# K K^T of chunks 6 to 11 in four-bank visits, the solve over two chunks, and U over four corners

## The chip, the core and the metric

The kernel runs on one core of a Trainium2 chip. The core has a matrix engine (TensorE, PE in the profile, with PEld for its weight loads), a vector engine (DVE), a scalar engine (ACT), GpSimd (POOL) and SyncE (SP), which here only issues DMAs; POOL issues DMAs too. Matmuls write to PSUM, which is handed out in banks of 128 x 512 fp32. The metric is the device time of one execution in microseconds, as the median of three runs.

## The reference

Four batches, eight heads, 768 tokens, heads of 48: a delta rule over the tokens, whose output, rearranged to 3072 x 384, goes through two MLPs.

```python
k_n = k / (norm(k) + 1e-06)
for t in range(S):
    y[:, :, t] = einsum('bhd,bhde->bhe', q[:, :, t], state)
    v_old = einsum('bhde,bhd->bhe', state, kt)
    state = state + bt * einsum('bhd,bhe->bhde', kt, vt - v_old)
x = y.transpose(0, 2, 1, 3).reshape(B * S, H * D)
h = np.maximum(x @ w_in, 0.0)                    # d_ff 2048
x = h * h @ w_out
h = np.maximum(np.maximum(x @ w1, x @ w2), x @ w3)   # d_ff 768
return h @ w_out2
```

## The kernel before

The tokens are cut into 12 chunks of 64 (`NC`). Within a chunk the delta rule is solved at once: K K^T of the chunk's keys, with beta, gives a triangular system of 64 x 64 per head, and its inverse is built from 32 x 32 blocks (the **solve**). All 32 heads are worked on together, in two halves p = 0 and 1 of eight pairs of heads (`U2` is 8; the two heads of a pair lie at partitions 0 to 63 and 64 to 127, t = 0 and 1). Chunks go in pairs: `HALVED[g]` is chunks 2g and 2g + 1, and the solve of a pair is done in one go, since 128 partitions hold both.

The MoE of a chunk, `moe_a(c)`, is the main stream of TensorE. For each of eight pairs of ff-tiles, `s1` does 18 matmuls 128 x 256 (L599), ACT and DVE square the result and split it into gh and gl (L605 to L608), and `s2` does 12 matmuls 128 x 384 (L619), two pairs later. `moe_a` yields after each s1 and each s2, and `steps` (L655 on) calls other generators at these yields by lists of numbers, the **slots**: 1 is behind s1(0), 2 behind s1(1), 3 behind s1(2), 4 behind s2(0), 5 behind s1(3), 6 behind s2(1), and so on by turns, to 12 behind s2(4), 13 behind s1(7), 14 behind s2(5), 15 behind s2(6), 16 behind s2(7) and the two DVE transposes of its sums (L639), which SP stores in the next chunk (`store_sums`, L652, the x stores). In the program's order these are the only places at which small work enters the stream. The orders of TensorE and DVE are pinned to the program's (`pin`); the queues of SP, ACT and POOL are laid out by the framework.

What is put into the slots of chunk c:

- `attention(c + 1)`, seven steps: load; A and Y from the state (`st0`, L467, 64 matmuls to each of two p, pA from pool `ps_at`, pY from `ps_y`); `zz` (L426); `ww` (L436); `mm_u`, the product U (L491, L494), whose result is copied to SBUF by ACT for p = 0 (L503) and by DVE for p = 1 (L501); `st2`, which adds P U to pY and gets the state's growth pD (L543, L521, L528, copies L553); and `st3`, transposes of the output (L561) that ACT and DVE split into xh and xl (L564, L565) for the next chunk's s1.
- `kkps`, K K^T of a pair of chunks, half by half: load of the keys (L169, 448 KB, two buffers in `buf` and `big`), `kk_matmul` (L172 to L182) into two banks pk and pq, copy by ACT (L198) and multiply by the mask on DVE (L199), stores kk (L186) and p (L206) to DRAM.
- `solve32` of the pair: loads of M from kk_d (L312), `prep` on DVE (L247 to L255, with a root on ACT, L218, and a select on POOL, L236), the transposed norms pt on TensorE (L279), 30 steps of two DVE instructions (L292, L293), the last multiply L296, and the stores of xt (L329), from which POOL loads xb and x for the attention.

K K^T of pair g stands in chunk 3, 5 and 7 for the pairs 3, 4 and 5 (`KK`), in four visits of two banks at slots 4, 6, 8 and 9. The solve's loads stand at slot 11, its prep at slot 15, and its steps in slots 1 to 14 of the next, even chunk. `ps_at` and `ps_y` have two banks each, px (two banks, sums of s2) and the two double banks of s1 take the others; U finds spare columns ("corners") of px and pY behind the 384 in use: four of eight heads of p = 0 lie in px, two of p = 1 in pY of p = 1.

Of the kernel before, what the change touches and what calls it, by code (L numbers as in the profile page):

```python
# [17 lines left out]
B, H, S, D = 4, 8, 768, 48  # L18
C = 64
# [4 lines left out]
DM = H * D  # L24
# [11 lines left out]
HALVED = [(c, c + 1) for c in range(0, NC, 2)]  # L36
U2 = 2 * Q


def delta_moe(ctx, tc, kc, ab, kt, vt, beta, beta32, beta16, kq, w_in, w_out, w1, w2, w3, w_out2, out):  # L40
    nc = tc.nc
    vec, act, pool = nc.vector, nc.scalar, nc.gpsimd
# [14 lines left out]
    ps_at = pp.enter_context(tc.tile_pool(name="ps_at", bufs=2, space=PSUM))  # L57
    ps_y = pp.enter_context(tc.tile_pool(name="ps_y", bufs=2, space=PSUM))
# [5 lines left out]
    mask = const.tile([128, C], F32, name="mask", tag="mask")  # L64
# [3 lines left out]
    p_d = [dram.tile([128, B * Q, C], F32, name=f"p{c}", tag=f"p{c}") for c in range(NC)]  # L68
# [82 lines left out]
    kcts, kss = [], []  # L151
# [7 lines left out]
    kcs, nk, kk_ends, mul_after, kc_after = {}, [0, 0], [None, None], [], []  # L159

    def two(d, c, p):

        return d[:, c, 2 * p:2 * p + 2]

    def kkp_load(c, p, dma=nc.sync):
        k = kcts[nk[0] % len(kcts)]
        nk[0] += 1
        kcs[c, p] = k
        i = dma.dma_start(k, two(kc, c, p).rearrange("p b q t s -> p (b q) t s"))  # L169
        for j in kc_after:  # L170
            behind(i.ins, j)

    def kk_matmul(c, p, ps_, swap=1):

        k = kcs.pop((c, p))
        pk, pq = (ps_[0].tile([128, U2, C], F32, name=n, tag=ps_[1]) for n in ("pk", "pq"))
        for u in range(U2):
            for i, ps in enumerate((pk, pq)):
                for t in range(2):
                    r = slice(64 * t, 64 * t + D)  # L180
                    o = 64 * (t ^ i * swap)
                    pe.matmul(ps[o:o + 64, u], k[r, u, 0], k[r, u, i], start=True, stop=True)  # L182
        return pk, pq

    def kk_store(c, p, kk, dma=nc.sync):
        dma.dma_start(kk_d[c // 2].rearrange("t j c u i -> (t j) c u i")[:, c % 2, U2 * p:U2 * p + U2], kk)  # L186

    def kkps(cs, ps_, dma=nc.sync):

        todo = [(c, p) for c in cs for p in range(2)]  # L190
        ahead = len(kcts) - (len(kcts) < 4)
        for n in range(min(ahead, len(todo))):
            kkp_load(*todo[n], dma)
        for n, (c, p) in enumerate(todo):
            ks = kss[nk[1] % len(kss)]
            nk[1] += 1
            pk, pq = kk_matmul(c, p, ps_[n % len(ps_)])
            kk_ends[0] = act.copy(ks[:, 0], pk).ins  # L198
            kk_ends[1] = vec.tensor_mul(out=ks[:, 1], in0=pq, in1=mask.unsqueeze(1).broadcast_to([128, U2, C])).ins  # L199
            for i in mul_after:  # L200
                behind(kk_ends[1], i)
            yield
            kk_store(c, p, ks[:, 0], dma)

            for t in range(2):
                dma.dma_start(p_d[c][64 * t:64 * t + 64, U2 * p:U2 * p + U2], ks[64 - 64 * t:128 - 64 * t, 1])  # L206
            if n + ahead < len(todo):
                kkp_load(*todo[n + ahead], dma)
            yield


    def norms(ss, n, u, pool_):

# [59 lines left out]
    def behind(ins, before):  # L273

        tc.add_manual_dep(ins, before.name, mybir.DependencyInfo(mybir.DependencyClass.NoSync, mybir.DependencyReason.DATA), reason="order")
# [115 lines left out]
    pxs = []  # L391
    ops, normed, norms_at, solved, solve_after = [], [], [], [], []

    def attention(c):
        xh[c] = wa.tile([128, KD, TB], F32R, name="xh", tag="xh", bufs=2)
        xl[c] = wa.tile([128, KD, TB], F32R, name="xl", tag="xl", bufs=2)
        half = lambda t: slice(64 * t, 64 * t + 64)
# [4 lines left out]
        def fresh(name, p, i, shape):  # L402
            t = att.tile(shape, F32, name=name, tag=name)
            tiles[c, p][i] = t
            return t


        merge, pYs = [], {}
# [69 lines left out]
        def mm_u(p):  # L478
            x, r = tiles[c, p][2], tiles[c, p][6]
            pU = ps_at.tile([128, U2, D], F32, name="pU", tag="at")  # L480
            own = p or c <= 2
            n = U2 - (0 if not c else 2 if own else 4)
            if c:
                free = pYs[p] if own else pxs
                over = free[0].rearrange("p (b n) -> p b n", b=1) if own else free[0]
                over = over[:, :, DM:DM + 2 * D].rearrange("p b (u d) -> p b u d", d=D)
            order = [u for i in range(U2) for u in (i, n + i) if (i < n if u == i else u < U2)]
            for u in order:
                for t in range(2):
                    if u < n:  # L490
                        pe.matmul(pU[half(t), u], x[half(t), u], r[half(t), u], start=True, stop=True)  # L491
                    else:
                        o = over[half(1 - t), (u - n) // 2, (u - n) % 2]
                        i = pe.matmul(o, x[half(t), u], r[half(t), u], start=False, stop=True, skip_group_check=True)  # L494
                        for j in free[1:]:
                            behind(i.ins, j)
            u_ = fresh("u", p, 7, [128, U2, D])
            on_vec = p and c != 1
            def put(to, po):
                if on_vec:  # L500
                    last_vec[0] = vec.tensor_copy(to, po).ins  # L501
                else:
                    last_act[0] = act.copy(to, po).ins  # L503
            put(u_[:, 0:n], pU[:, 0:n])
            if held and c < 2:
                masked(p)
            if c:
                for m in range(n, U2, 2):
                    for t in range(2):
                        put(u_[half(t), m:m + 2], over[half(1 - t), (m - n) // 2])  # L510

        yy, pDs = {}, {}

# [218 lines left out]
    if True:  # L732
# [14 lines left out]
        for t in range(2):  # L747
            m = mask[64 * t:64 * t + 64]
# [44 lines left out]
        at, p1 = (ps_at, "at"), (ps_s1, "p1")  # L793
# [11 lines left out]
        for c in range(2):  # L805
            for x in range(4):
                j = (pool if c else nc.sync).dma_start(halves[0][32 * x + 16 * c:32 * x + 16 * c + 16], beta32[c, 16 * x:16 * x + 16]).ins
# [63 lines left out]
        for n, (c, p) in enumerate(todo):  # L871
            pg = pw[:, 1].rearrange("p (u s) -> p u s", s=C) if n == 1 else bank((sy, None, p1, at)[n])
            grams(n, 1, [pg] * 2)
            ks = kss[n][:, 1] if c else tiles[c, p][3]
# [87 lines left out]
        KK = {1: 2, 3: 3, 5: 4, 7: 5}  # L962
        ahead_ = {}
        for c in range(NC):
            extra = []
            if c == 0:
                solve_next = solve32(1, (pool, pool))
                extra += [(11 / 15.0, later(3, attention(1))), (list(range(17)), weights(2, 2)), (4.0, later(20, part(solve_next, 10)))]
            elif c == 1:
                pinned.update({first_matmul.ins.engine: None, last_gl[0].engine: None})  # L970
                first_solve = [0] * 3 + [1 + n * 18 // 20 for n in range(20)]
                extra += [(first_solve, solve_next), ([13, 19, 22, 25, 27, 28, 30], attention(2))]
                ahead_[2] = solve32(2, landing=1)
                extra += [([9, 10, 16, 17, 20, 21, 24, 25], kkps(HALVED[2], (at,))), ([28], ahead_[2], True)]
                solve_after[:] = last_vec
                kc_after[:] = raws[-1:]
                prep_after.clear()
            elif c + 1 < NC:
                extra.append(([1, 2, 5 + c // 9, 7 + c // 9, 10, 12, 14] if c % 2 else [1, 2, 4, 6, 8, 11, 13], attention(c + 1)))
            if c == 2:  # L980
                kc_after.clear()
                solve_after.clear()
            if c in ahead_:
                extra.append(([2] + [3 + n * 12 // 32 for n in range(32)] if c == 2 else [1 + n * 14 // 32 for n in range(32)], ahead_[c]))
            if c > 1 and c in KK:
                extra.append(([4, 5, 6, 7, 8, 9, 9, 10], kkps(HALVED[KK[c]], (at,))))
                ahead_[c + 1] = solve32(KK[c], landing=1)
                extra.append(([11, 15], ahead_[c + 1], True))
            if c == 9:
                after[:] = last_gl  # L990
                load_w3s = w3load((0, 1))
            if 9 <= c < NC - 1:
                extra.append((0.4, part(load_w3s, 6)) if c > 9 else (0.8, later(6, part(load_w3s, 6))))
            if c == NC - 1:
                pr.close()
                wb = ctx.enter_context(tc.tile_pool(name="wb", bufs=1, side="right", reuse_waits="tile"))
                first = []
                extra.append((0.6, chain(load_w3s, w3load((2,)))))
                extra.append((0.5, later(2, x2_steps(0, wb, first))))
            steps(moe_a(c, gp, c == 1), *extra)  # L1000
# [114 lines left out]
```

## Time and profile before

| | |
|---|---|
| median of three runs | 906.56 us (905.05 to 907.78) |
| profiled execution | 903.85 us, span 902.1 us, mean granted clock 0.977 |
| PE busy | 868.1 us (96%) |
| DVE busy | 479.4 us (53%) |
| ACT busy | 387.7 us (43%) |
| POOL busy | 135.8 us (15%) |
| chunk 7 of the MoE (with K K^T) | 47.41 us |
| chunk 9 (without) | 42.21 us |

The attention with chunk 0 and the load of the weights take the first 120 us or so, the chunks of the MoE run to 597 us, and the second MLP follows. The shares are means over these stages; what a microsecond is worth in one is read from that stage's own waits.

### The profile page before, as it was taken

Reading aid. Unit: us, or ns where it says so; the run is one execution under the profiler, and the core shown is the slowest. Engines: PE = TensorE matmul, PEld = TensorE weight load, DVE = VectorE, ACT = ScalarE, POOL = GpSimd, SP = SyncE. Lnnn points to the kernel's source line nnn. Section 1 sums busy time; section 2 is a strip of 40 time slices with the busy share of each in tenths; the row PEclk is TensorE's granted clock in tenths of the full one; section 3 lists DMA queues with packets and bytes.
Section 4 is the critical chain, followed back from the end, with each engine's and each line's share of the span. In section 5 each row is a group of like instructions: output and inputs, shape, how many; then the busy total and the mean of one; then the engine's idle time right before and its main releaser. Section 6 shows DMA issues by size and latency. Waiting matters only on the chain.

```text
span 902.1 us, 26366 instructions
## 1 busy us (share of the span) xinstructions
PE 868.1 (96%) x11414; PEld 843.6 (94%) x11414; DVE 479.4 (53%) x1069; ACT 387.7 (43%) x825; POOL 135.8 (15%) x226
## 2 busy tenths in 40 slices
PE   5589999999999999999999999999999999999998
PEld 5478989999999999999999999999999999999997
DVE  5988885695378437843784545556232332323221
ACT  5558745354445444534453755644121221212111
POOL 4140200322312241224123300011000000000000
PEclk8659999999999999999999999999999999999999
DMA  9977436725742585257427431444010110000000
GB/s 258 361 184 225 132 89 176 153 65 140 194 112 66 144 191 110 66 145 159 100 66 171 118 92 38 127 111 136 20 36 27 36 37 25 10 27 9 18 18 35
DMA packets 114035, 95.36 MB, mean 106 GB/s; under 512 B 69880, under 2 KB 95240, under 8 KB 113920
## 3 DMA queue, kind: packets, MB, share of 16 engines
q1 hardware_dynamic: 95232, 55.41, 23.8%
q0 software_dynamic: 11584, 32.64, 13.7%
q10 hardware_dynamic: 7104, 5.64, 2.1%
q8 instruction: 89, 1.46, 0.7%
q14 instruction: 26, 0.21, 0.1%
HBM read 70.45 MB, written 22.77 MB: 103 GB/s over the span
## 4 chain that ended last, share of the span: by engine, by line
PE 86%; DVE 6%; ACT 3%; DMA 3%; issue 2%; POOL 0%; DVEq 0%; ACTq 0%; POOLq 0%
PE p L1023 25%; PE p L599 21%; PE px L619 20%; PE po L1040 8%; PE pY L543 2%; PE pU L491 2%; PE pk L182 1%; PE pA L467 1%; DMA p<-ksr 1%; PE pW L436 1%; PE pZ L426 1%; DVE gl L608 1%; PE pT L561 1%; DMA ktp<-in_kt_dram 1%; PE pq L182 1%
## 5 line engine op out<-in xcount | busy, mean ns | idle before, releaser
L1023 PE MATMUL p<-x_h,w 128*128 128x384 f32 x864 | 220.1, 336 | 0.0
L619 PE MATMUL px<-wout,gh 128*128 128x384 f32 x768 | 198.6, 339 | 1.4 <-ACT gh L607 1.4
L599 PE MATMUL p<-xh,win_h 128*128 128x256 f32 x576 | 169.6, 294 | 1.9 <-DVE gl L608 1.4
L599 PE MATMUL p<-xl,win_h 128*128 128x256 f32 x576 | 163.8, 284 | 0.2 <-DVE xl L565 0.2
L599 PE MATMUL p<-xh,win_l 128*128 128x256 f32 x576 | 163.7, 284 | 0.0
L1023 PEld LDWEIGHTS p<-x_h,w 128*128 128x128 f32 x864 | 156.3, 188 | 0.0
L1023 PE MATMUL p<-x_l,w 128*128 128x384 f32 x432 | 145.3, 336 | 0.0
L608 DVE TENSOR_TENSOR gl<-p,gh 128x512 fp32r<-128x512 f32 x96 | 66.3, 690 | 142.3 <-ACT gh L607 141.9
L619 PEld LDWEIGHTS px<-wout,gh 128*128 128x128 f32 x768 | 134.5, 189 | 2.6 <-ACT gh L607 1.5
L619 PE MATMUL px<-wout,gl 128*128 128x384 f32 x384 | 128.8, 335 | 0.0
L605 ACT ACTIVATE p<-p 128x512 f32<-128x512 f32 x96 | 55.9, 583 | 165.1 <-PE p L599 162.6
L599 PEld LDWEIGHTS p<-xh,win_h 128*128 128x128 f32 x576 | 110.6, 192 | 5.8 <-DVE gl L608 2.3
L599 PEld LDWEIGHTS p<-xl,win_h 128*128 128x128 f32 x576 | 110.8, 192 | 0.5 <-DVE xl L565 0.4
L599 PEld LDWEIGHTS p<-xh,win_l 128*128 128x128 f32 x576 | 110.9, 192 | 0.0
L1029 DVE TENSOR_TENSOR mx<-p,mx 128x384 f32<-128x384 f32 x48 | 26.7, 557 | 126.2 <-PE p L1023 126.1
L1023 PEld LDWEIGHTS p<-x_l,w 128*128 128x128 f32 x432 | 81.3, 188 | 0.0
L1031 ACT CAST hh<-mx 128x384 fp32r<-128x384 f32 x48 | 24.6, 514 | 125.4 <-DVE mx L1030 125.2
L619 PEld LDWEIGHTS px<-wout,gl 128*128 128x128 f32 x384 | 72.1, 188 | 0.0
L293 DVE TENSOR_TENSOR buf<-buf 128x30 f32<-128x30 f32 (+9 forms) x180 | 59.7, 332 | 6.1
L292 DVE TENSOR_TENSOR buf<-buf 128x30 f32<-128x30 f32 (+9 forms) x180 | 59.3, 330 | 4.8
L607 ACT CAST gh<-p 128x512 fp32r<-128x512 f32 x96 | 56.3, 587 | 2.5
L606 ACT ACTIVATE p<-p 128x512 f32<-128x512 f32 x96 | 56.0, 583 | 2.6
(169 smaller groups left out, 1309.2 us busy)
## 6 DMA issues: line engine op xcount, KB each, us to landing
kq<-in_kc_dram POOLq DMA_DIRECT2D x20, 448.0 KB, 5.4
raw<-in_moe_w_dram SPq DMA_DIRECT2D x18, 384.0 KB, 3.8
raw<-in_moe_w_out_dram SPq DMA_DIRECT2D x16, 384.0 KB, 3.8
p<-p POOLq DMA_DIRECT2D x22, 256.0 KB, 4.0
rawp<-in_moe_w_in_dram SPq DMA_DIRECT2D x12, 384.0 KB, 6.5
v<-in_vt_dram POOLq DMA_DIRECT2D x24, 192.0 KB, 3.9
ktp<-in_kt_dram POOLq DMA_DIRECT2D x24, 192.0 KB, 4.1
x<-xs SPq DMA_DIRECT2D x48, 96.0 KB, 3.2
```

What stands on the lines that cost most here:

```text
L292: eng.tensor_tensor(out=tv, in0=col.unsqueeze(2).broadcast_to([u, k, l]), in1=row.unsqueeze(1).broadcast_to([u, k, l]), op=ALU.mult)
L293: i = eng.tensor_tensor(out=of_, in0=of_, in1=tv, op=ALU.add)
L599: pe.matmul(p1[:, j], w[:, k, f], x[c][:, k], start=n == 0 and j == 0, stop=n == 8, skip_group_check=True)
L605: act.activation(out=p1, in_=p1, func=AF.Relu)
L606: act.activation(out=p1, in_=p1, func=AF.Square)
L607: last_gh[0] = act.copy(gh, p1).ins
L608: last_gl[0] = vec.tensor_sub(out=gl, in0=p1, in1=gh.bitcast(F32)).ins
L619: g = pe.matmul(px[:, h, 0:DM], x[:, j, hs], w, start=f == 0 and i == 0, stop=f == NF - 1 and i == 2, skip_group_check=True)
L1023: pe.matmul(p, w[i][:, k, fs], x[:, k], start=n == 0, stop=n == 8)
L1029: vec.tensor_max(out=t, in0=ps[1], in1=t)
L1031: act.copy(hh[:, f], t2)
L1040: pe.matmul(po[:, 0:DM], x[:, f, js], w[:, f], start=i == 0, stop=i == 17)
```

## The change

A new generator, `kk_twos`, does K K^T of one chunk in one visit: both halves' keys are loaded, both `kk_matmul` follow one another, p = 0 into the two banks of `ps_at` and p = 1 into those of `ps_y`, then come the copies and multiplies, and at the next call the stores and the loads for the pair's second chunk. The first chunk of a pair is done at slot 15 of the even chunk ahead (its keys are loaded at slot 8), the second at slot 2 of the odd chunk, ahead of A, which moves from slot 2 to 4 there. The solve's loads move from slot 11 to 6 and prep from 15 to 9; seven steps of the solve follow in slots 10 to 16, the others in slots 1 to 12 of the even chunk. pt, which was called at slot 4 with zz, is now called at slot 1. In `mm_u` of p = 1, from chunk 3 on, four of the eight heads go to corners: two in pY of p = 0 and two in pY of p = 1.

```diff
+    def kk_twos(cs):
+        for c in cs:
+            for p in range(2):
+                kkp_load(c, p)
+            yield
+            staged = []
+            for p, ps_ in enumerate(((ps_at, "at"), (ps_y, "y"))):
+                staged.append((kss[nk[1] % len(kss)], *kk_matmul(c, p, ps_)))
+                nk[1] += 1
+            for ks, pk, pq in staged:
+                act.copy(ks[:, 0], pk)
+                vec.tensor_mul(out=ks[:, 1], in0=pq, in1=mask.unsqueeze(1).broadcast_to([128, U2, C]))
+            yield
+            for p, (ks, _, _) in enumerate(staged):
+                kk_store(c, p, ks[:, 0])
+                for t in range(2):
+                    nc.sync.dma_start(p_d[c][64 * t:64 * t + 64, U2 * p:U2 * p + U2], ks[64 - 64 * t:128 - 64 * t, 1])
+        yield
...
-            own = p or c <= 2
-            n = U2 - (0 if not c else 2 if own else 4)
-            if c:
-                free = pYs[p] if own else pxs
+            free = [] if not c else [pYs[p]] if c <= 2 else [pYs[0], pYs[1]] if p else [pxs]
...
+            n = U2 - 2 * len(overs)
...
-                extra.append(([1, 2, 5 + c // 9, 7 + c // 9, 10, 12, 14] if c % 2 else [1, 2, 4, 6, 8, 11, 13], attention(c + 1)))
+                extra.append(([1, 2, 6, 8, 10, 12, 14] if c > 8 and c % 2 else [1, 4, 6, 8, 10, 12, 14] if c % 2 else [1, 2, 4, 6, 8, 11, 13], attention(c + 1)))
...
-                extra.append(([2] + [3 + n * 12 // 32 for n in range(32)] if c == 2 else [1 + n * 14 // 32 for n in range(32)], ahead_[c]))
+                extra.append(([2] + [3 + n * 12 // 32 for n in range(32)] if c == 2 else [1 + n * 12 // 25 for n in range(25)], ahead_[c]))
+            if c > 1 and c + 1 in KK:
+                two_by_two = kk_twos(HALVED[KK[c + 1]])
+                extra.append(([8, 15, 16], two_by_two, True))
             if c > 1 and c in KK:
-                extra.append(([4, 5, 6, 7, 8, 9, 9, 10], kkps(HALVED[KK[c]], (at,))))
+                extra.append(([2, 3], two_by_two))
                 ahead_[c + 1] = solve32(KK[c], landing=1)
-                extra.append(([11, 15], ahead_[c + 1], True))
+                extra.append(([6, 9, *[10 + n for n in range(7)]], ahead_[c + 1], True))
```

The new lines push the others down: L295 on stand 20 lines lower in the new file, `mm_u` and what follows 21.

SP's queue at the end of chunk 2 and the start of chunk 3, before; the first row is the last of four stores of xt (the solved pair 2), x are the sums of chunk 2, kk and p the products of chunk 6. A number in square brackets is the semaphore of a queue or an engine that is waited for.

```order
L329 DMA xt_113<-buf 32x1024 [waits DMAHW1_49]
L652 DMA x_120<-xs 768x1x32 [waits DMAHW2_49,DVE_49]
L652 DMA x_120<-xs 768x1x32 [waits DMAHW3_49]
L652 DMA x_120<-xs 768x1x32 [waits DMAHW4_49]
L652 DMA x_120<-xs 768x1x32 [waits DMAHW5_49]
L169 DMA buf<-in_kc_dram 112x1024 [waits DMAHW6_49,PE_49]
L186 DMA kk_96<-buf 128x512 [waits DMAHW7_49,Activation_49]
L206 DMA p_105<-buf 64x512 [waits DMAHW0_49,DVE_49]
L206 DMA p_105<-buf 64x512 [waits DMAHW1_49]
```

The same place after:

```order
L349 DMA xt_113<-buf 32x1024 [waits DMAHW1_49]
L186 DMA kk_96<-buf 128x512 [waits DMAHW2_49,Activation_49]
L229 DMA p_105<-buf 64x512 [waits DMAHW3_49,DVE_49]
L229 DMA p_105<-buf 64x512 [waits DMAHW4_49]
L186 DMA kk_96<-big 128x512 [waits DMAHW5_49,Activation_49]
L229 DMA p_105<-big 64x512 [waits DMAHW6_49,DVE_49]
L229 DMA p_105<-big 64x512 [waits DMAHW7_49]
L169 DMA buf<-in_kc_dram 112x1024 [waits DMAHW0_49,PE_49]
L169 DMA big<-in_kc_dram 112x1024 [waits DMAHW1_49,PE_49]
L673 DMA x_120<-xs 768x1x32 [waits DMAHW2_49,DVE_49]
```

The stores of both halves of chunk 6 now follow the stores of xt, behind them stand the two loads of chunk 7, and the stores of x come later.

DVE in chunk 3, from the copies of U (L501) to the first row of prep (L247), before; ss, s, r and a are prep's small tiles:

```order
L501 COPY u<-pU 128x288 [waits PE_49]
L501 COPY u<-pY 64x96 x2
L608 TENSOR_TENSOR gl<-p_3778,gh 128x512 [waits PE_49,Activation_49]
L528 TENSOR_TENSOR Sb<-pD,Sb 128x384 [waits PE_49] x2
L553 COPY yy<-pY 64x4x48 x4
L608 TENSOR_TENSOR gl<-p_3914,gh 128x512 [waits DVE_49,PE_49,Activation_49]
L565 TENSOR_TENSOR xl<-pT,xh 128x3x128 [waits Activation_49] x2
L247 COPY ss<-buf 128x32 [waits DMAHW6_49,DMAHW7_49,DMAHW1_49,DMAHW0_49]
```

After, from the end of prep (its multiply by r, L257, and L275) on:

```order
L257 TENSOR_TENSOR buf<-buf,r 128x1024 [waits DVE_49,Pool_49]
L275 TENSOR_SCALAR a_3625<-r 128x32
L522 COPY u<-pU 128x192 [waits PE_49]
L522 COPY u<-pY 64x96 x2
L522 COPY u<-pY 64x96 [waits PE_49]
L522 COPY u<-pY 64x96
L312 TENSOR_TENSOR buf<-buf 128x30 [waits DVE_49]
L313 TENSOR_TENSOR buf<-buf 128x30 [waits DVE_49]
L629 TENSOR_TENSOR gl<-p_3807,gh 128x512 [waits PE_49,Activation_49]
```

Prep stood behind xl; now it stands ahead of the copies of U, which are five in place of three, and of gl.

TensorE at the start of `st2` of p = 0, in chunk 3, before (u are the copied U, p the masked products):

```order
L543 MATMUL pY<-u,p 64x48 [waits DMASW1_49]
L543 MATMUL pY<-u,p 64x48
L521 MATMUL pD<-u,ktp_136 64x48 [waits DMASW2_49,PE_49]
L521 MATMUL pD<-u,ktp_136 64x48
L543 MATMUL pY<-u,p 64x48 x2
```

After:

```order
L564 MATMUL pY<-u,p 64x48 [waits DMASW1_49,DVE_49]
L564 MATMUL pY<-u,p 64x48
L542 MATMUL pD<-u,ktp_136 64x48 [waits DMASW2_49,PE_49]
L542 MATMUL pD<-u,ktp_136 64x48
L564 MATMUL pY<-u,p 64x48 x2
```

The first matmul into pY, which waited for one load alone, waits for DVE too.

## Rows read from the trace of the kernel before

**Rows 1.** The page, busy time (us, share, instructions) of each engine.

```profile
PE 868.1 (96%) x11414; PEld 843.6 (94%) x11414; DVE 479.4 (53%) x1069; ACT 387.7 (43%) x825; POOL 135.8 (15%) x226
```

**Rows 2.** By stretch, chunks 7 and 9: length; PE, PEld, DVE, ACT, POOL; clock, DMA.

```profile
388.54:435.95 47.41, 47.41 (x952) 45.09 (x952) 18.62 (x37) 21.40 (x45) 16.87 (x27) 1.00 0.72 163
...
478.23:520.44 42.21, 42.21 (x697) 40.80 (x696) 19.06 (x40) 24.05 (x50) 15.55 (x26) 1.00 0.62 155
```

**Rows 3.** PE's timeline (start, length) around A, K K^T and U.

```profile
392.56 0.28 PE L599 MATMUL p<-xl,win_h 128*128 128x256 f32 x1
...
395.01 0.28 PE L599 MATMUL p<-xh,win_l 128*128 128x256 f32 x1
...
398.96 0.34 PE L619 MATMUL px<-wout,gl 128*128 128x384 f32 x1
...
400.54 0.28 PE L599 MATMUL p<-xh,win_l 128*128 128x256 f32 x1
...
456.61 0.34 PE L619 MATMUL px<-wout,gl 128*128 128x384 f32 x1
...
458.40 0.28 PE L599 MATMUL p<-xh,win_l 128*128 128x256 f32 x1
```

**Rows 4.** PE's timeline: the last s2 of chunk 2, A in chunk 3.

```profile
207.04 0.51 PE L619 MATMUL px<-wout,gh 128*128 128x384 f32 x2
...
213.52 0.26 PE L467 MATMUL pA<-Sb,kq 48*64 48x48 f32 x2
```

**Rows 5.** DVE's timeline at the end of chunk 2.

```profile
206.51 1.01 DVE L565 TENSOR_TENSOR xl<-pT,xh 128x384 fp32r<-128x384 f32 x2
```

**Rows 6.** SP's queue (start, time of the issues), chunks 3 and 7.

```profile
210.31 1.72 SPq L329 DMA_DIRECT2D xt<-buf  x4
...
413.85 0.34 SPq L186 DMA_DIRECT2D kk<-buf  x1
...
414.28 1.09 SPq L206 DMA_DIRECT2D p<-buf  x2
```

**Rows 7.** Loads to landing: L169 of the whole run; kq, 205 to 235 us.

```profile
DMA to landing us min/median/max: 3.6/4.0/8.5
...
kq<-in_kc_dram POOLq DMA_DIRECT2D x2, 448.0 KB, 6.1
```

**Rows 8.** PE's timeline ahead of chunk 2: instructions behind a wait [length, releaser].

```profile
27.99 0.48 PE L182 MATMUL pk<-buf 48*64 48x64 f32 x4 [11.28 <-DMA buf<-in_kc_dram]
...
58.19 0.69 PE L561 MATMUL pT<-ident,yy 128*128 128x128 f32 x3 [1.70 <-ACT yy L555]
...
73.46 0.62 PE L619 MATMUL px<-wout,gh 128*128 128x384 f32 x2 [1.36 <-ACT gh L607]
```

**Rows 9.** By stretch, as in rows 2, after and around two of these waits.

```profile
28.00:34.50 6.50, 6.50 (x122) 6.50 (x124) 5.98 (x16) 1.31 (x3) 0.00 (x0) 0.50 1.04 337
...
58.00:59.00 1.00, 0.69 (x3) 0.31 (x3) 0.94 (x4) 0.22 (x2) 0.74 (x2) 0.72 0.86 176
```

**Rows 10.** DVE's timeline: prep's first and last in chunk 7; gl in chunk 9.

```profile
432.95 0.18 DVE L247 COPY ss<-buf 128x32 f32<-128x32 f32 x1
...
437.42 0.18 DVE L255 TENSOR_SCALAR a<-r 128x32 f32<-128x32 f32 x1
...
503.23 0.69 DVE L608 TENSOR_TENSOR gl<-p,gh 128x512 fp32r<-128x512 f32 x1 [4.41 <-ACT gh L607]
```

**Rows 11.** PE's timeline: U and st2 in chunk 7, U in chunk 9.

```profile
418.88 0.26 PE L491 MATMUL pU<-v,xb 64*64 64x48 f32 x2
...
424.61 0.26 PE L543 MATMUL pY<-u,p 64*64 64x48 f32 x2
...
503.37 0.26 PE L491 MATMUL pU<-v,xb 64*64 64x48 f32 x2
```

**Rows 12.** DVE's copies of U by shape: count | busy, mean ns | idle before.

```profile
L501 DVE COPY u<-pY 64x96 f32<-64x96 f32 x20 | 5.1, 254 | 0.3
...
L501 DVE COPY u<-pU 128x288 f32<-128x288 f32 x10 | 4.5, 454 | 4.9 <-PE pU L491 4.8
```

More of the change, by code (lines that the diff above doesn't have):

```diff
@@ L480, in mm_u @@
             pU = ps_at.tile([128, U2, D], F32, name="pU", tag="at")
-            own = p or c <= 2
-            n = U2 - (0 if not c else 2 if own else 4)
-            if c:
-                free = pYs[p] if own else pxs
-                over = free[0].rearrange("p (b n) -> p b n", b=1) if own else free[0]
-                over = over[:, :, DM:DM + 2 * D].rearrange("p b (u d) -> p b u d", d=D)
+            free = [] if not c else [pYs[p]] if c <= 2 else [pYs[0], pYs[1]] if p else [pxs]
+            overs, held_by = [], []
+            for tile_, *before in free:
+                flat = tile_.rearrange("p (b n) -> p b n", b=1) if len(tile_.shape) == 2 else tile_
+                overs += [flat[:, b, DM:DM + 2 * D].rearrange("p (u d) -> p u d", d=D) for b in range(flat.shape[1])]
+                held_by += before
+            n = U2 - 2 * len(overs)
             order = [u for i in range(U2) for u in (i, n + i) if (i < n if u == i else u < U2)]
@@ L492, in mm_u @@
                     else:
-                        o = over[half(1 - t), (u - n) // 2, (u - n) % 2]
+                        o = overs[(u - n) // 2][half(1 - t), (u - n) % 2]
                         i = pe.matmul(o, x[half(t), u], r[half(t), u], start=False, stop=True, skip_group_check=True)
-                        for j in free[1:]:
+                        for j in held_by:
                             behind(i.ins, j)
@@ L509, in mm_u @@
                     for t in range(2):
-                        put(u_[half(t), m:m + 2], over[half(1 - t), (m - n) // 2])
+                        put(u_[half(t), m:m + 2], overs[(m - n) // 2][half(1 - t)])
         yy, pDs = {}, {}
```

## The prediction

> **What bounds the kernel now.** First the busy times of the engines [rows 1]: TensorE works 868 us, 96% of the span. Then the span by chunks of the MoE [rows 2]: in chunk 7 and in chunk 9 its busy time is the whole length of the stretch, with the granted clock at 1.00; the other chunks from 3 to 10 read alike. So from chunk 3 on, no wait is left to gain there, and the only gain is fewer or denser matmuls. A microsecond taken out of TensorE's own work shortens the span by one, and a new wait of TensorE lengthens it by one. DVE, ACT and the queues have room on average; the question is only where one of them is late at one place. Chunk 9 has no K K^T: 47.41 - 42.21 = 5.20 us are what the four visits of chunk 7 cost.
>
> **What is saved.** A visit is a batch of small tiled matmuls between the large ones. I take its price as the distance between the large ones around it, less their own steady step (0.12 for L599, 0.175 for L619) [rows 3]. K K^T in two banks: 400.54 - 398.96 - 0.29 = 1.29 us; four of them make 5.16, in agreement with the 5.20. A over both p, which is a four-bank visit with twice the steps: 395.01 - 392.56 - 0.24 = 2.21 us. So 16 more steps cost 0.92 us (0.0575 each) and 0.37 us belongs to the visit. Two four-bank visits of K K^T make 4.42: a saving of 0.74 a pair, 2.2 us for three pairs. That a visit changes its operand tile midway costs nothing extra, since the A visit does so too. U: 458.40 - 456.61 - 0.29 = 1.50 us, about 20 steps, of which the second pair has twelve, because only two of its eight heads lie in spare corners. With four in corners it has eight: 4 x 0.0575 = 0.23 us, in the nine attentions 3 to 11: 2.1 us. **Saved in all: 4.3 us.**
>
> **What is added on TensorE.** pt, the transpose of the norms, stood with zz and now stands alone in the slot list of chunks 4, 6 and 8. It is one matmul, bounded by nothing and by a visit's 0.37 us; being one plain matmul, it is nearer to the large ones than to a batch of tiled ones, so I take 0.1, 0.3 us in all.
>
> **Wait 1, chunk 2.** The first four-bank visit stands at slot 15, ahead of the last s2, which began at 207.04 [rows 4]; less the 0.23 saved in U, TensorE is there at about 206.8. The second bank of pk and pq is that of the last pT, which DVE gives back with the second xl, at 206.51 + 1.01 = 207.52 [rows 5]. DVE is full with the solve there, and the four corner copies (below) push it 0.2 to 0.4 later. Wait 0.5 to 1.1; I take 0.8. In chunks 4 and 6 less of the solve is left and I put nothing.
>
> **Wait 2, the largest: chunk 7's keys, in chunk 3.** SP's new order (first pair of fences in the section on the change) has the four stores of xt, then six stores of chunk 6, and behind them both loads of chunk 7. xt waits for the last multiply of the solve, which sets 210.31 before [rows 6], and with DVE as above 210.4 to 210.7. Four stores of xt take 1.72 us; one kk and its two p take 0.34 + 1.09 and the gap, 1.5 us, twice. So the loads are issued at 210.5 + 1.8 + 3.1 = 215.4 and 215.8. A load of this line lands 3.6 us after issue at the least, 4.0 in the median, 8.5 at most [rows 7]: 219.4 and 219.8, while POOL's loads of kq, at 6.1, share the time. TensorE is due at slot 2 of chunk 3, where A began at 213.52 [rows 4]; plus 2.21 for the visit of chunk 6, plus wait 1, less 0.23: 216.2 to 216.4. It waits 219.4 - 216.2 = **3.2 us** (2.7 with 3.6, 7 with 8.5). A and every matmul of the chunk are queued behind. In the old order one load stands there, behind the stores of xt and x alone, and its matmuls came at slot 4. In the pairs 4 and 5 the load of the odd chunk's first half stands directly behind the matmuls that free its buffer, with no xt stores close ahead; by the same durations it lands 2 to 3 us before it is wanted, so nothing there.
>
> **What that wait does to the clock.** TensorE waited 1.70 us before 58.19 and 1.36 before 73.46 [rows 8]. After the first, the granted clock fell within 58 to 59 (mean 0.72, between 1.00 and 0.50); after the second it did not. After the long wait that ended at 27.99 [rows 8] it was 0.50 for 6.5 us of unbroken work [rows 9]. 0.50 is 1.2 GHz of 2.4. A wait of 3.2 us is nearer to the first and third, so I take it to fall, and 6.5 us at that level to give back some 3.2 us less than at the full one, since a few of the instructions are bound otherwise: 3.0 us (0 where it doesn't fall; up to 4). The Trainium skill (TensorE: Matmul & The Clock Gate, HAM oscillation) tells of a kernel in which each wait for a DMA between two bursts of matmuls put the clock to half, so that the next burst began slow. By that rule the 3.0 us stand; without it the sum would be 3.0 lower.
>
> **Wait 3, chunks 3, 5 and 7.** The prep of the next solve runs on DVE from 432.95 to 437.60, 4.6 us, behind everything of chunk 7 [rows 10]. It moves to slot 9, in DVE's order ahead of the copies of the second U (second pair of fences). Take U's first matmul as zero. In chunk 9, where no K K^T lies in between, the gl ahead ends at 503.92, 0.55 after U began at 503.37 [rows 10, 11]. Prep then ends at 5.2, the copy of pU at about 5.5 (0.45 for 288 columns, now 192), the two of the first pY's corners 0.51 later [rows 12], at 6.0. The first matmul of st2 came at 424.61 - 418.88 = 5.73 [rows 11], now 5.50. It is the first pY that it adds to, so it now waits for these copies (the third pair of fences shows the new wait on DVE): 0.5 us, three times, 1.5 us (0 to 2.5). Before, DVE was done with U 2 us after it began. The Trainium skill (PSUM — Partial Sum Buffer, section PSUM bank collisions raise a hardware error) says to guard PSUM by bank and quadrant, not by address, which speaks against the corners: the columns that st2 writes are others than those being copied. Guarded by address the sum would be 1.5 us lower; the order shows the wait, and no run here shows its length yet.
>
> The other moves cost nothing as far as the rows tell: ACT's copies of pk are one for one, the solve's multiplies are the same number, and no row shows TensorE waiting for the solve.
>
> **The sum.** -2.2 - 2.1 + 0.3 + 0.8 + 3.2 + 3.0 + 1.5 = +4.5 us. The profiled execution took 903.85 us (span 902.1), which becomes 908.4; it lies 2.7 below the median of 906.56, so I forecast 911.1 for the median. About 0.3% (2.7 us) is what a measurement of this kernel can tell from no change.
>
> **Rivals.** (a) The wait for chunk 7's keys comes, but the clock stays at 1.00: +1.5, 908.1, no change that can be measured. For it speaks the 1.36-us wait; against it the other two, which were in stretches where TensorE was less busy ahead. (b) Faster: the keys are there when wanted and prep is off DVE before U's copies, so that the visits' savings are what is left: -4.3 + 0.3 + 0.8 + 0.3 = -2.9, 903.7. It decides where the loads leave SP by 212.5, 3 us ahead of my reckoning; the durations of the stores speak against it. (c) Slower still: pairs 4 and 5 wait for their second visit too, because their loads run beside stores, xb and kq and land at 6 us and more, not at 4: then 2 us and a clock fall each, up to 10 us more; one of them gives 916. The margin of 2 to 3 us and the maximum of 8.5 [rows 7] are its point. (d) The four-bank visit is no cheaper than two visits: 2.2 us more, 913.3; the A visit speaks against it.
>
> **Chances.** Forecast 0.38 (its own range 909 to 913.5), (a) 0.27, (b) 0.18, (c) 0.12, (d) 0.05. Slower by over 0.3%: forecast, (c) and (d), 0.55; within 0.3%: (a) with the edge of (b), 0.28; faster 0.17. The range 903.5 to 915.5 leaves some 0.1 out on either side.
>
> **What would show it.** Chunk 3 should have one TensorE wait of about 3 us before L182's pk, released by the DMA of the keys, with a granted clock under 1.00 right behind it; chunks 3, 5 and 7 a wait of about 0.5 us before st2's first pY, released by DVE's copies of u; chunk 2 one of under 1 us before pq, released by xl. The pure work should move: chunk 7, with one visit in place of four, to 42.21 + 2.21 - 0.23 = 44.2 us without its waits, and chunk 9 to 42.0. The forecast is wrong if chunk 3 has no wait or keeps its clock, or if chunks 5 and 7 wait for keys too.

## The result, and the profile after

The changed kernel takes 914.23 us (median of 6 runs, 913.12 to 916.92) and the kernel before, beside it, 904.83 (6 runs): a ratio of 1.0111, with a 95% interval of 1.0095 to 1.0126. It is slower, as forecast, and near the upper end of the range, above the 909 to 913.5 of the forecast itself; the movement, 9.4 us in the medians and 10.1 us between the profiled spans, is about twice the 4.5 of the sum.

The page of the changed kernel, as in [rows 1]: the span has grown by 10.1 us, the busy time of PE only by 2.8 (part of that is work at a lower clock). What came is waiting.

```profile
span 912.2 us, 26395 instructions
...
PE 870.9 (95%) x11414; PEld 846.4 (93%) x11414; DVE 480.5 (53%) x1087; ACT 387.6 (42%) x825; POOL 134.7 (15%) x226
```

The same by stretch, as in [rows 2], for chunks 3, 7 and 9 of the changed kernel (length; PE, PEld, DVE, ACT, POOL; clock, DMA share, GB/s):

```profile
211.46:266.99 55.53, 47.70 (x823) 45.56 (x823) 21.59 (x52) 20.49 (x43) 16.75 (x27) 0.91 0.66 153
...
401.23:446.21 44.98, 44.58 (x823) 42.72 (x823) 21.41 (x52) 20.31 (x43) 11.85 (x19) 1.00 0.60 148
...
488.29:530.29 42.00, 42.00 (x696) 40.60 (x696) 19.46 (x42) 24.02 (x50) 12.18 (x21) 1.00 0.53 127
```

Cut in that way at the first s1 of each chunk, both kernels stand like this (us; "reckoned" is the chunk before, less the four visits of two banks where there were any, plus 2.21 for a four-bank visit, less 0.23 for U):

| chunk | 2 | 3 | 4 | 5 | 6 | 7 | 8 | 9 | 10 |
|---|---|---|---|---|---|---|---|---|---|
| before | 43.41 | 47.42 | 42.21 | 47.42 | 42.21 | 47.41 | 42.28 | 42.21 | 42.19 |
| reckoned | 45.39 | 44.19 | 44.19 | 44.19 | 44.19 | 44.19 | 42.05 | 41.98 | 41.96 |
| after | 46.25 | 55.53 | 44.31 | 45.62 | 44.31 | 44.98 | 42.08 | 42.00 | 42.20 |

Chunk 3 alone loses 11.3 us against the reckoning. The waits of TensorE from 100 to 620 us (what waited, for what; us in all, times, longest; the main rows) say for what:

```profile
PE pk L182 <- DMA buf<-in_kc_dram: 7.2, 1, 7.2
PE pY L564 <- DVE u L522: 1.2, 3, 0.4
PE pT L582 <- DVE Sb L549: 1.1, 2, 0.6
...
PE pk L182 <- DMA big<-in_kc_dram: 0.6, 2, 0.3
```

Its place on PE's timeline, and the granted clock around it (columns as above, the clock is the eleventh number, ahead of DMA share and GB/s):

```profile
223.08 0.37 PE L182 MATMUL pk<-buf 48*64 48x64 f32 x2 [7.16 <-DMA buf<-in_kc_dram]
```

```profile
219.00:220.00 1.00, 0.00 (x0) 0.00 (x0) 0.00 (x0) 0.00 (x0) 0.00 (x0) 0.86 0.94 279
...
223.00:224.00 1.00, 0.92 (x34) 0.95 (x38) 0.00 (x0) 0.00 (x0) 0.00 (x0) 0.50 0.93 184
...
229.00:230.00 1.00, 1.00 (x7) 1.00 (x7) 0.00 (x0) 0.00 (x0) 0.00 (x0) 0.52 1.05 332
```

TensorE stood still from 215.92 to 223.08. The clock fell at about 219.7 and came back just before 230, so that the first 6.9 us behind the wait went by at 0.50 (1.2 GHz of 2.4). SP's queue ahead of it, where [rows 6] stood for the durations:

```profile
209.98 1.96 SPq L349 DMA_DIRECT2D xt<-buf  x4
212.04 0.37 SPq L186 DMA_DIRECT2D kk<-buf  x1
212.50 1.13 SPq L229 DMA_DIRECT2D p<-buf  x2
213.72 0.54 SPq L186 DMA_DIRECT2D kk<-big  x1
214.35 1.49 SPq L229 DMA_DIRECT2D p<-big  x2
215.93 0.53 SPq L169 DMA_DIRECT2D buf<-in_kc_dram  x1
216.56 0.39 SPq L169 DMA_DIRECT2D big<-in_kc_dram  x1
```

The keys left SP at 215.93, half a microsecond later than reckoned, and landed not 4.0 but 7.0 us after:

```profile
buf<-in_kc_dram SPq DMA_DIRECT2D x1, 448.0 KB, 7.0
```

Prep and the copies of U came as reckoned. DVE and PE in chunk 3, as in [rows 10, 11]; time zero of the reckoning is 249.75:

```profile
249.61 0.69 DVE L629 TENSOR_TENSOR gl<-p,gh 128x512 fp32r<-128x512 f32 x1 [4.43 <-ACT gh L628]
...
254.70 0.17 DVE L275 TENSOR_SCALAR a<-r 128x32 f32<-128x32 f32 x1
254.78 0.35 DVE L522 COPY u<-pU 128x192 f32<-128x192 f32 x1
255.15 1.07 DVE L522 COPY u<-pY 64x96 f32<-64x96 f32 x4
```

```profile
249.75 0.26 PE L512 MATMUL pU<-v,xb 64*64 64x48 f32 x2
...
255.72 0.32 PE L564 MATMUL pY<-u,p 64*64 64x48 f32 x4 [0.39 <-DVE u L522]
```

Prep ends at 254.87, 5.1 us after U began, and st2 starts 5.97 after it. The reckoning had 5.2 and 6.0, and 5.50 for a st2 that isn't held up.

### The profile page after: what moved, and what is told of

Same layout as the page of the kernel before. It is cut to its first block, busy times and chain, and to the rows that moved or that the text cites. A ratio compares the mean times of both kernels' runs of the same rounds, so it can differ in the third digit from the quotient of the medians.

```text
span 912.2 us, 26395 instructions
## 1 busy us (share of the span) xinstructions
PE 870.9 (95%) x11414; PEld 846.4 (93%) x11414; DVE 480.5 (53%) x1087; ACT 387.6 (42%) x825; POOL 134.7 (15%) x226
## 4 chain that ended last, share of the span: by engine, by line
PE 81%; DVE 8%; DMA 5%; ACT 3%; issue 2%; SPq 0%; ACTq 0%; DVEq 0%
PE p L1047 25%; PE p L620 19%; PE px L640 18%; PE po L1064 8%; PE pk L182 2%; DMA big<-in_kc_dram 1%; PE pA L487 1%; PE pY L564 1%; PE pW L456 1%; PE pq L182 1%; PE pU L512 1%; PE pZ L446 1%; DMA kct<-in_kc_dram 1%; DMA buf<-in_kc_dram 1%; DVE gl L629 1%
```

## The experiments

Only the edits are shown, as differences from the changed kernel where nothing else is said. Times of one comparison are held against the kernel before in that comparison.

**Keys on POOL's queue, first form (e1, e2, e4).** The loads of the second chunk's keys are issued on POOL, behind the matmuls that free their buffers.

```diff
+            if not n:
+                key_loads.clear()
+                for p in range(2):
+                    key_loads.append(kkp_load(cs[1], p, pool))
             yield
...
+    def queued(to, src):
+        i = pool.dma_start(to, src)
+        for j in key_loads:
+            behind(i.ins, j)
```

`queued` takes the place of `pool.dma_start` in `load_x`, so that these loads stay behind the keys.

The rewritten loop had lost a `yield`: the second visit moved from slot 2 of the odd chunk to slot 16 of the even one, one s2 behind the first. All three runs have that in common.

> The change whole, but the loads of the second chunk's keys go out on POOL's queue straight behind the matmuls that free their buffers, ahead of that queue's loads of xb; SP keeps the stores. Theory (the keys are late because SP issues them behind four stores of xt and six of kk and p, at 215.93): they are issued near 208.5 and 209.5, land by 216 even at 7 us, TensorE's wait in chunk 3 is under 0.5 us, the granted clock stays 1.00, chunk 3 falls from 55.5 to about 45 us, and the time is about 11 us under the changed kernel's, 903 where the kernel before has 904.8. Rival 1 (contention: the keys land late whenever they are issued): still a wait of 2 us or more in chunk 3, 907 or more. Rival 2 (the four-bank visits themselves or the other moves cost it): chunk 3 stays over 50 us.

Measured: 924.29 against 904.88 us (ratio 1.0211, 1.0189 to 1.0232).

> As the run before, and the solve back at its old slots: loads of M at 11, prep at 15, all steps in the even chunk. Theory (prep holds DVE and so the copies of U, 0.4 us of wait before st2 in chunks 3, 5 and 7): these three waits go, 1.2 us less, about 902. Rival (the wait comes from the two more corner copies alone): the waits stay, no change.

Measured: 921.06 (ratio 1.0187, 1.0165 to 1.0209).

> The kernel before with K K^T in four-bank visits alone (keys of the second chunk on POOL's queue), the solve at its old slots, U as it was. Theory: 0.74 us less a pair, 2.2 us, less 0.5 to 0.9 us of wait for a bank in chunk 2: 903.2 to 903.6 where the kernel before has 904.8. Rival (a four-bank visit is no cheaper than two of two banks): 904.8 to 905.7.

Measured: 919.78 (ratio 1.0175, 1.0161 to 1.0188). What the expectations say of the time can't be read from these runs: chunk 3 was free of the wait, but each pair now waited 1.4 to 3.7 us in the even chunk, where its keys had been asked for only 1.5 to 3 us ahead. The lists of waits can: e1 has three waits of st2 for u, 1.2 us in all, and e2, with prep late, has none. And the clock shows something else. The shortest wait, in e4 at chunk 2, with 0.34 us more in the middle of the visit, and the clock behind it:

```profile
212.79 0.27 PE L191 MATMUL pk<-buf 48*64 48x64 f32 x2 [1.42 <-DMA buf<-in_kc_dram]
```

```profile
212.00:214.00 2.00, 1.16 (x64) 1.05 (x64) 0.45 (x1) 0.00 (x0) 0.00 (x0) 1.00 1.02 356
214.00:215.00 1.00, 0.71 (x43) 0.74 (x47) 0.00 (x0) 0.00 (x0) 0.21 (x1) 0.93 1.01 377
215.00:218.00 3.00, 3.00 (x42) 2.88 (x37) 0.44 (x1) 0.58 (x1) 3.00 (x6) 0.50 0.85 273
218.00:219.00 1.00, 1.00 (x9) 1.00 (x8) 0.25 (x1) 0.59 (x1) 1.00 (x2) 0.87 0.91 270
```

Behind the wait of 1.42 us (with the 0.34) out of a stretch of full work the clock was down for 3.4 us, but not at once: the next matmuls began at 1.00, and it fell some 2 us later. Behind the others, of 1.9 to 3.7 us, it was down for 3 to 7. In all three pairs of all three kernels it fell. Other waits left it at 1.00: the 0.34 us that the changed kernel has in chunk 5, those of 1.0 to 1.1 us in f1 and f2, and one of 1.47 us for copies of u in g1 (these runs follow).

**Keys on POOL's queue, second visit at slot 2 (f1).** The same with the `yield` put back:

> The change whole, with the keys of the second chunk on POOL's queue, straight behind the matmuls that free their buffers; the second visit stays at slot 2 of the odd chunk (in e1, e2 and e4 my edit had moved it to slot 16 of the even chunk, where its keys had only been asked for, and so each pair waited 2 to 3.5 us). Theory (the changed kernel loses 11 us by keys that leave SP late, and by the clock after): keys issued near 208.5 and 209.5 land by 215, TensorE is due at 216, no wait, clock 1.00, chunk 3 at 44.6 to 45.1 us, time 902.5 to 904 where the kernel before has 904.9. Rival (the keys land late wherever they are queued, since xt, kk, p and x move at the same time): a wait over 1.5 us in chunk 3 and 906 or more.

Measured: 903.86 against 904.01 us (ratio 0.9994, 0.9983 to 1.0005). The keys leave earlier, in POOL's queue, and the first load lands in 4.3 us:

```profile
209.44 0.55 POOL L169 DMA_DIRECT2D buf<-in_kc_dram  x1 [10.04 <-PE pq L191]
210.37 0.53 POOL L169 DMA_DIRECT2D big<-in_kc_dram  x1 [0.39 <-PE pq L191]
...
buf<-in_kc_dram POOLq DMA_DIRECT2D x1, 448.0 KB, 4.3
```

and TensorE's work goes through; the first of these rows by stretch is where the changed kernel stood still, the second is chunk 3:

```profile
215.00:220.00 5.00, 5.00 (x153) 4.80 (x153) 1.98 (x3) 4.01 (x8) 4.55 (x8) 1.00 0.93 293
212.19:258.70 46.51, 44.56 (x823) 42.56 (x823) 21.59 (x52) 20.30 (x43) 17.36 (x28) 1.00 0.67 180
```

Ten microseconds come back by one edit that touches only when and by whom the keys are asked for (POOL's own loads of xb, behind them, leave 3 us later than in the changed kernel). The work of chunk 3 is 44.56 us in a length of 46.51: what is left are 0.85 us before st2 and 1.10 us for which the profile names no releaser; the profiled execution was the slowest of the twelve, at 906.3. So the theory stands, and neither the four-bank visits nor the other moves cost anything of that size. f1 doesn't part the earlier moment from the other queue; the first load of f6, below, does.

**Prep at its old place (f2).** f1 with the solve as in the kernel before:

```diff
-                extra.append(([2] + [3 + n * 12 // 32 for n in range(32)] if c == 2 else [1 + n * 12 // 25 for n in range(25)], ahead_[c]))
+                extra.append(([2] + [3 + n * 12 // 32 for n in range(32)] if c == 2 else [1 + n * 14 // 32 for n in range(32)], ahead_[c]))
...
-                extra.append(([6, 9, *[10 + n for n in range(7)]], ahead_[c + 1], True))
+                extra.append(([11, 15], ahead_[c + 1], True))
```

> As the run before, and the solve at its old slots (loads of M at 11, prep at 15, all steps in the even chunk). Theory: the three waits of 0.4 us before st2 go, 1.2 to 1.5 us under the run before. Rival (the waits come from the corner copies, whoever is ahead of them): the same time as the run before.

Measured: 901.60 us (ratio to the kernel before 0.9961, 0.9945 to 0.9976), 2.3 us under f1. No wait for u is left in its list; chunks 5 and 7 take 44.63 and 44.22 us. That is a little more than the 1.2 to 1.5 expected; f1's profile has one more wait of 1.0 us with no releaser, in chunk 5, which f2's hasn't. With f4, below, this is the fastest of all, and faster than both kernels.

**K K^T alone (f3).** f2 with `mm_u` as in the kernel before:

> The kernel before with four-bank visits of K K^T alone, at the changed kernel's slots, keys on POOL, solve and U as before. Theory: 0.74 us less a pair, less the wait for a bank in chunk 2: 902.7 to 903.7 where the kernel before has 904.9; pairs of chunks 4 and 5, and 6 and 7, at 88.8 to 89.0 us in place of 89.63. Rival (no cheaper by the visit): 89.6 a pair of chunks and 904.9.

Measured: 903.79 us (ratio 0.9994, 0.9982 to 1.0005). By chunks the saving is there: chunks 4 and 5 take 44.45 + 44.52 = 88.97 us, 6 and 7 take 88.88, where before they took 89.63. So a four-bank visit costs 2.24 us, where 2.21 were reckoned. With the 0.33 of chunks 2 and 3 that makes 1.7 us. The time doesn't show it: 0.2 us less by the medians, and at most 1.6 by the interval, with executions from 900.16 to 905.78. The time that was expected is missed.

**U over four corners alone (e3).** The kernel before with the changed `mm_u`:

> The kernel before with nothing changed but U of the second pair over four corners. Theory: 0.23 us a visit in nine chunks, 2.1 us less, with up to 0.4 us given back in chunk 2, where DVE is full: 902.9 to 903.3 where the kernel before has 904.8, chunks 8 and 9 at 42.05 and 42.0. Rival (st2 now waits for the copies of the first pY's corners everywhere, as a guard by bank would have it): no gain, 904.8 or more.

Measured: 904.41 against 904.88 us (ratio 0.9996, 0.9988 to 1.0005). Chunks 4 to 9 take 0.22 to 0.28 us less each, as expected, but chunk 2 takes 43.87, 0.46 more, and chunks 3 and 10 0.1 more: 0.7 us less in the nine chunks, where 2.1 were reckoned. The time is 0.5 us less, not the 1.5 to 1.9 expected. No wait of st2 appears, so the rival falls too: with prep elsewhere the copies are done in time.

**Corners left out where they seemed to lose (f4).**

```diff
-            free = [] if not c else [pYs[p]] if c <= 2 else [pYs[0], pYs[1]] if p else [pxs]
+            free = [] if not c else [pYs[p]] if c <= 2 or p and c in (3, NC - 1) else [pYs[0], pYs[1]] if p else [pxs]
```

> As f2, with the four corners left out of the attentions 3 and 11, which e3 showed to lose 0.46 us in chunk 2 and to gain nothing in chunk 10. Theory (the corner copies cost where DVE is full, in chunk 2 by the solve and in chunk 10 by the next weights): 0.5 to 0.8 us under f2, 901 to 901.8. Rival (those losses have another cause): as f2.

Measured: 901.70 us (ratio 0.9976, 0.9966 to 0.9986), the same as f2, as the rival had it. By chunks the theory is right in chunk 2 and wrong in chunk 10. Chunk 2 falls from 46.28 to 46.08, and pT's wait of 0.4 us for Sb is gone there. Chunk 10 rises from 41.98 to 42.19: there the corners gain in f2, and the loss that e3 showed in chunk 10 was of that profile only.

**Keys on SP, further ahead (f5, f6).** Is it SP's order that makes them late, or what moves at that time? f5 puts both loads in the middle of the six stores, f6 puts the first ahead of them.

```diff
             for p, (ks, _, _) in enumerate(staged):
+                if p and not n:
+                    for i in range(2):
+                        kkp_load(cs[1], i)
                 kk_store(c, p, ks[:, 0])
```

That is f5; f6 has the two loads ahead of the `yield` before this loop.

> The change whole, the keys on SP as there, but both loads stand in the middle of the six stores of kk and p (three ahead of them, three behind). They leave SP near 213.7 and 214.2 in place of 215.93 and 216.56. Theory (SP's order sets the wait, landing takes 7 us while the stores move): TensorE's wait falls from 7.2 to about 4.9 us, the clock still falls, and chunk 3 takes 52 to 53 us in place of 55.5. Rival (landing takes the 4.0 us of the other loads, and the 7 us were bad luck): a wait of about 2 us, chunk 3 under 50.

Measured (one run): 912.55 against 906.30 us. The keys left SP 2.4 us after chunk 3 began, in place of 4.5, and TensorE still waited 6.63 us; chunk 3 took 54.16. The landing, to set beside the 7.0 of the changed kernel:

```profile
buf<-in_kc_dram SPq DMA_DIRECT2D x1, 448.0 KB, 8.5
```

What was gained in the queue was lost on the way. My theory that SP's order sets the wait falls in this form, and so does the rival's landing of 4.0.

> As the run before, but the first load stands ahead of the six stores, behind those of xt alone, and the second behind the first kk and p (the framework's order). They leave SP near 212.0 and 213.6. Theory: the first keys land near 217 to 219, a wait of 1 to 3 us, the second 1 to 2 us later; the clock falls where the two waits come to 2 us and more; chunk 3 at 46 to 50 us. Rival (landing 4.0): no wait to speak of, chunk 3 at 45.

Measured (one run): 908.02 against 906.30 us; chunk 3 took 51.23. The first keys left at 211.03 and were there 4.3 us later; the second left at 212.54, behind one store of kk and one of p, and came 7.5 us later:

```profile
215.28 0.27 PE L182 MATMUL pk<-buf 48*64 48x64 f32 x2 [0.36 <-DMA buf<-in_kc_dram]
...
220.17 0.37 PE L182 MATMUL pk<-big 48*64 48x64 f32 x2 [3.73 <-DMA big<-in_kc_dram]
```

The first load did what the rival said, from SP's own queue: early enough, it is there in time. The second was worse than either had it, and chunk 3 is above both forecasts. The 1.7 us over the kernel before are less than its single executions differ by.

**The stores behind the keys (g1).** The keys keep their place in SP's queue, but the six stores ahead of them move one pair of heads in eight, and six more, behind the keys, the other seven.

```diff
+            def store(us):
+                for p, (ks, _, _) in enumerate(staged):
+                    o = slice(U2 * p + us.start, U2 * p + us.stop)
+                    nc.sync.dma_start(kk_d[c // 2].rearrange("t j c u i -> (t j) c u i")[:, c % 2, o], ks[:, 0, us])
+                    for t in range(2):
+                        nc.sync.dma_start(p_d[c][64 * t:64 * t + 64, o], ks[64 - 64 * t:128 - 64 * t, 1, us])
+            if c == cs[0]:
+                store(slice(0, 1))
```

The other seven (`1:`) are stored by the same lines right behind the loads of the keys.

> The change whole, the keys at their place on SP behind the stores of xt and six stores of kk and p; but of the products of chunk 6 (and 8 and 10) these six move only one head pair in eight, and six more behind the loads of the keys move the rest, so that 0.9 of 1.05 MB stand behind the keys and not ahead of them. Theory (the bytes moving at that time, 3 MB in 12 us at 200 to 280 GB/s, make the keys take 7 us; what stands behind them shares the DMA engines too): the keys leave SP near 215 and still take 6 us and more, wait 5.5 to 7 us, chunk 3 at 53 to 55.5. Rival 1 (only what is ahead counts): landing 4 to 5 us, wait near 4 us, chunk 3 at 51 or less. Rival 2 (the time of issue alone counts): wait of 6.5 to 7 with a landing as before, only if the issue is not earlier.

Measured (one run): 913.94 against 903.79 us; chunk 3 took 53.35. The issue, the landing and the wait:

```profile
215.80 0.53 SPq L169 DMA_DIRECT2D buf<-in_kc_dram  x1
```

```profile
buf<-in_kc_dram SPq DMA_DIRECT2D x1, 448.0 KB, 4.7
```

```profile
220.59 0.37 PE L183 MATMUL pk<-buf 48*64 48x64 f32 x2 [4.41 <-DMA buf<-in_kc_dram]
```

Left at the same moment, the keys land in 4.7 us and not 7.0, and the wait is 4.41 and not 7.16. That is the landing and the wait of the first rival: what is ahead of them counts. So of the 7.2 us, 4.4 remain with the time of issue and a landing of 4.7, and 2.7 go with the 0.9 MB of stores that were on their way, by one execution. Chunk 3 stays over that rival's 51, since the clock fell here too and was at 0.50 for 6.3 us. (The whole kernel gained nothing, since chunk 5 took 47.15 in this run, and st2 waited for copies of u up to 1.5 us.)

Could it have been the stores of x, which follow right behind the keys in SP's queue, and which g1 moves back too? They go in pieces of 128 B. In the changed kernel 119 packets under 512 B moved from 217 to 222.9, while the keys were on their way, and 2549 from 222.9 to 226: the stores of x came after the keys.

## Why the prediction was right, and where it was off

**What bounds the kernel**: right. TensorE has no slack from chunk 3 on; a saving of a few tenths shows in each chunk, a new wait at full length.

**Saved, 4.3 us.** K K^T: right by the chunks, 0.66 and 0.74 us in f3 for the second and third pair, where 0.74 was reckoned, and 0.33 in the first, whose visit in chunk 2 takes longer. U: the 0.23 a visit is right (chunks 8 and 9 lose 0.20 and 0.21), but not in all nine chunks. Chunk 2 became 0.46 longer in e3 in place of 0.23 shorter: pT waits some 0.4 us for Sb on DVE there, in every kernel with four corners in that chunk, and in none without. The term was 2.1 and is 0.7 by chunks of e3.

**pt alone**: 0.1 a chunk reckoned; chunk 4 takes 44.31 with it alone and 44.23 in f2, where it stands with zz: 0.08. Chunk 8 shows none of it (42.08 and 42.10).

**Wait 1, 0.8 us in chunk 2**: chunk 2 lost 0.86 against the reckoning, but by another row. The second xl ended at 207.20, and the visit was hardly held: it took 2.39 us by the large matmuls around it, 0.18 over the 2.21. The rest, 0.66, was lost earlier, at pT, with 0.41 of it as a wait for Sb. The same cause (DVE late by the copies of U) came out one step ahead of where it was looked for; f4, without these corners, hasn't got the wait.

**Wait 2, 3.2 us: the mis-sized term.** It measured 7.16: 0.5 from an issue at 215.93, 0.3 from TensorE being there at 215.92, and 3.0 from a landing in 7.0 us. The step that failed is taking the median landing of [rows 7] for a load that leaves behind 1 MB of stores just issued. The same row had 8.5 as its other end, and the range held for that reason (with 8.5 the prediction's own terms make a wait of 7.7, not the 7 that it gives). Luck helped as well: the forecast was added to a median of three, 906.56, where the six executions have 904.83. From there its own range would be some 907.3 to 911.8 and the outer one end at 913.8, and 914.23 would lie outside. The movement, not the time, is the measure, and it was twice the forecast. The changed kernel's DMA engines by stretch (columns as above; DMA share and GB/s come last):

```profile
205.00:209.00 4.00, 4.00 (x134) 3.75 (x135) 3.73 (x14) 0.58 (x1) 0.00 (x0) 1.00 0.00 0
209.00:211.00 2.00, 2.00 (x31) 1.93 (x23) 2.00 (x3) 0.59 (x1) 0.00 (x0) 1.00 0.18 39
211.00:213.00 2.00, 2.00 (x17) 2.00 (x16) 1.20 (x3) 0.00 (x0) 0.51 (x1) 1.00 0.90 214
213.00:215.00 2.00, 2.00 (x19) 2.00 (x18) 0.00 (x0) 1.16 (x2) 2.00 (x5) 1.00 0.88 253
```

They move nothing up to 209 and are at 0.9 of their time from 211 on. In f1 the keys leave from 209.44 on, in the second of these, 1.3 us ahead of the first store of xt (210.71) and 3 us ahead of the first of kk (212.58).

**The clock, 3.0 us**: right in kind, and near in size: 6.9 us at half behind the wait where 6.5 were reckoned, which cost 3.5 by what is left of chunk 3's 11.3 when the waits (7.16, 0.29 for the second half's keys, 0.39 before st2) are taken off. The rule of the Trainium skill (TensorE: Matmul & The Clock Gate, HAM oscillation), by which the burst behind such a wait begins slow, held for the changed kernel, whose burst at 223.08 began at 0.50. In the runs as a whole the clock fell for all thirteen waits for keys of 1.4 us and more, but only in six of them was it down when the burst began; in the other seven it fell 0.2 to 2.3 us later. Rival (a) falls by that.

**Wait 3, 0.5 us three times**: 0.39, 0.39 and 0.40, as rows show it, and gone in f2. The rule of the Trainium skill (PSUM — Partial Sum Buffer, section PSUM bank collisions raise a hardware error) agrees with the order of this kernel: st2 waited for copies of other columns of the bank that it writes. What would come without that wait no run shows.

**Rivals.** (b), all waits absent: f2 is that case, reached by other means, at 2.4 us under the kernel before by the medians and 3.5 by its interval's middle, where 2.9 were reckoned. (c), keys late in pairs 4 and 5 too: only 0.34 us, in chunk 5, though its 916 is nearer to the measured time than the forecast's 911.1. (d), no cheaper visit: refuted by the chunks of f3.

What stays open: chunk 5 is 1.43 us longer than reckoned, and its two waits, 0.39 before st2 and 0.34 for the second half's keys, explain half of it; 0.30 more lies in the visit of A behind them, which takes that much longer than in f2 with no wait listed. Chunk 10 is 0.24 longer, and nearly all of that is at its visit of A, where a wait of 0.16 has no releaser.

## What to carry to other kernels

Where the main engine has no slack, a saving in its work is worth what it measures, and any transfer that the change puts later must be priced with the bytes that are on their way ahead of it, not by a median landing (4.3 to 4.7 us against 7.0 to 8.5 here); look for the stretch in which the DMA engines are idle and ask for the data there. A wait of TensorE out of full work can cost more than its length: here 3 to 7 us at half clock lay behind every wait for keys of 1.4 us and more, and none behind the waits of 1.0 to 1.1 us and a single one of 1.47. And a long piece on DVE is harmless until it is moved ahead of a copy that the next matmul needs.

## What was not expected of the hardware

How long a load of 448 KB took went with the stores of kk and p issued just ahead of it, but not in proportion: 4.3 us with none (f1, and the first of f6), 4.7 with 0.13 MB (g1), 7.5 with 0.4 MB and another load of keys (the second of f6), 8.5 with 0.5 MB (f5), and 7.0 with 1.05 MB (the changed kernel). The DMA engines were at 0.9 of their time in f1 as well, so that share doesn't tell the two apart. Why f5's is the longest these runs don't explain. And in f1 TensorE stood for 1.1 us with no releaser in the profile, while the DMA engines were at 0.85 and more of their time:

```profile
228.33 0.39 PE L633 MATMUL p<-xh,win_l 128*128 128x256 f32 x1 [1.10 <-issue]
```

It comes in f2 at the same place and not in the changed kernel, f3 or f4. What it waits for was not found.
